# Loads moved to GpSimd's queue, pooled rows in two DRAM tensors, filling rows dropped

## The chip, the cores and the metric

One NeuronCore of a Trainium2 chip. The metric is the device time of one execution in microseconds (us); of several runs the median counts. TensorE does matmuls, transposes among them; VectorE (DVE), ScalarE (ACT) and GpSimd (POOL) work elementwise; SyncE (SP) only issues transfers here. SP, ScalarE and GpSimd can each issue DMAs, which run on the core's 16 DMA engines. Every engine takes its own instructions in order, a DMA issue among them, and waits on semaphores.

## The reference

Inputs are q, k and v of 8 batches, 8 heads, 576 positions and 64 columns (f32), a gate vector, and two matrices of 512 x 1024 and 1024 x 512.

```python
q_d, k_d, v_d = (x.reshape(B, H, S // 4, 4, D).mean(axis=3) for x in (q, k, v))
out_up = np.repeat(sm_attn(q_d, k_d, v_d), 4, axis=2)            # coarse attention, 144 rows
mask = np.abs(pos[:, None] - pos[None, :]) < 4
out_local = softmax(where(mask, scale * q @ k.T, -1e9)) @ v      # local attention
x = (out_up + out_local)  as (B, S, H * D)
scores = einsum("bsd,d->bs", x, w_gate)
for b in range(B):
    top_idx = the 128 rows with the largest scores[b]
    xe = x[b, top_idx]
    ye = np.maximum(xe @ w1, 0) @ w2
    out[b, top_idx] = xe + sigmoid(scores[b, top_idx])[:, None] * ye
```

Each batch has a coarse attention (every pooled row is used for four positions), a local one within three positions, their sum, and a two-layer network on the 128 best rows, which are read from and written back to the output by index.

## The kernel before, in words

The batches run through a software pipeline. Each step of a batch is a Python generator; `put` gives it a place in time in units of a batch (the table `PLACE`), and all pieces are written into the program in the order of these places. The tile framework then sets the semaphores, chooses buffers and orders the instructions of an engine again by its own estimate. Instructions that go through the helper `InOrder` (lines 48 to 55; the names `sp`, `aq`, `vq`) are pinned behind the instruction that the program last gave to the same engine; the profile records them all as line 55.

The steps of batch b:

- `load_qk` (line 169) loads q and k transposed into the tile T in two halves of 1152 KB, more than a batch ahead. `pool_qk` (178) sums groups of four columns on VectorE.
- `pool_v` (202) loads vraw, 1152 KB, and sums groups of four rows on GpSimd (207, 209), into vd; vr (213) follows. `load_vw` (192) loads the windows of v for the local attention in three transfers, two of 520 KB and one of 260 KB.
- `coarse` (223) has two units: scores (237), exponent (262), transposes (275), product (296 to 311). It ends with the tile ods (319): 128 partitions with 512 columns for the first 128 pooled rows, and 64 columns more in which partition h * 16 + c holds row 128 + c of head h. ods is written to the DRAM tile up_d, each row four times: one transfer for the first 128 rows (323) and four, one for each repetition, for the last 16 (328). Then VectorE works out gate scores from ods (332, 336).
- `load_up` (347) reads up_d back as the tiles x: 128 partitions are two blocks of 58 positions, padded to 64 rows each. It has three groups of tiles (0 and 1, 2 and 3, 4) and seven transfers, one of which brings ten rows that fill tile 4 up to 128 partitions.
- `local` (380) has three units: scores (407), maximum (416), exponent (423), transposes (429), product with vw (441), division (451) into the tile t, gate scores (456).
- `sums` (466) adds t to x on GpSimd (469) and stores x to the output, twelve transfers a batch on SP's queue.
- `route` (481) ranks the 576 scores, makes the list idx (528) of the best 128 and gathers these rows (536) from the output into xe, on GpSimd's queue. It runs while the next batch is in its coarse and local steps.
- `moe` (555) multiplies by the two matrices in f16 pairs (564 to 568, 581 to 583), and a scatter (587), also from GpSimd, writes the rows back.
- `load_weights` (142) loads the matrices in eight pieces through the tile stg during the first batch and a half; ScalarE and VectorE convert each piece (146, 147).

All loads of inputs except the first constants are issued by ScalarE (`aq`), all writes and reads of up_d and all stores by SP (`sp`), the gathers and scatters by GpSimd.

Of the kernel before, what the change touches and what calls it, by code (L numbers as in the profile page):

```python
# [11 lines left out]
F32 = mybir.dt.float32  # L12
# [4 lines left out]
ALU = mybir.AluOpType  # L17
# [41 lines left out]
def tile_multires_attention_moe(ctx: ExitStack, tc: tile.TileContext, qk, vw, vp, cs, w_gate, w1, w2, outs):  # L59
# [2 lines left out]
    nc = tc.nc  # L62
    B, _, _, HP, S = qk.shape
    pool = nc.gpsimd
    sp, aq, vq = (InOrder(tc, e) for e in (nc.sync, nc.scalar, nc.vector))
    D = P // 2
    H = 2 * HP
    DM = H * D
# [44 lines left out]
    def load_constants():  # L113
        n = at["first"]
        sp.dma_start(out=cst[:, :n], in_=cs[:, :n])
        for t in (*qzbuf, *pzbuf, first):
            pool.memset(t, 0.0)
        pool.memset(ones, 1.0)
        nc.vector.tensor_copy(identb, ident)
        nc.vector.tensor_copy(mask.rearrange("p e t k -> p (e t k)"), const("mask"))  # L120
        for t in vals:
            nc.vector.tensor_copy(t[:, :, 0], const("tok"))
        nc.vector.tensor_copy(pen, const("pen"))
        nc.vector.tensor_copy(off, const("off"))
        yield
        aq.dma_start(out=wg, in_=w_gate.unsqueeze(0).broadcast_to([P, DM]))
        aq.dma_start(
            out=wgr, in_=w_gate.rearrange("(h d) -> h d", d=D).unsqueeze(1).broadcast_to([H, SR, D])
        )
        aq.dma_start(out=cst[:, n:], in_=cs[:, n:])  # L130
        pool.tensor_copy(first[:, :P], const("first"))
        yield

# [3 lines left out]
    w2l = cpool.tile([P, NF, DM], F16, name="w2l")  # L137

    x_d = outs
    up_d = [dpool.tile([SD, FACTOR, DM], F32, name=f"up_d{b}") for b in range(B)]  # L140

    def load_weights():
        pend = []

        def convert(sv, h_, l_):
            aq.activation(h_, sv, AF.Copy, scale=WS)
            vq.scalar_tensor_tensor(out=l_, in0=sv, scalar=WS, in1=h_, op0=ALU.mult, op1=ALU.subtract)

        for src, hi, lo, n in ((w1, w1h, w1l, DF), (w2, w2h, w2l, DM)):
            for i in range(4):  # L150
                cc = hi.shape[1] // 4
                stg = ld.tile([P, 4 * 256], F32, tag="stg", name="stg", bufs=4)
                sv = stg.rearrange("p (c f) -> p c f", f=n)
                aq.dma_start(
                    out=sv, in_=src[i * cc * P : (i + 1) * cc * P, :].rearrange("(c p) f -> p c f", p=P)
                )
                cs_ = slice(i * cc, (i + 1) * cc)
                pend.append((sv, hi[:, cs_, :], lo[:, cs_, :]))
                if len(pend) == 4:
                    convert(*pend.pop(0))  # L160
                yield
        while pend:
            convert(*pend.pop(0))
            yield
# [4 lines left out]
    def load_qk(b):  # L169
        qkT[b] = wk.tile([P, 2, HP, S], F32, tag="T", name=f"T{b}")  # L170
        hh = HP // 2
        for u in range(2):
            aq.dma_start(
                out=qkT[b][:, :, hh * u : hh * (u + 1)], in_=qk[b][:, :, hh * u : hh * (u + 1)]
            )
            yield
# [15 lines left out]
    def load_vw(b):  # L192
        vwin[b] = []
        for i, tiles in enumerate(TU):
            t = wk.tile([P, 2 * len(tiles), HP, D1], F32, tag=f"vw{i}", name=f"vw{b}_{i}", bufs=1)
            aq.dma_start(out=t, in_=vw[b][:, 2 * tiles[0] : 2 * tiles[-1] + 2])
            vwin[b].append(t)
            yield

# [1 line left out]

    def pool_v(b):
        raw = ld.tile([P, FACTOR, DM + D], F32, tag="vraw", name="vraw", bufs=2)
        aq.dma_start(out=raw, in_=vp[b])
        yield
        vd = vds[b] = wk.tile([P, DM + D], F32, tag="vd", name=f"vd{b}")
        pool.tensor_tensor(out=vd, in0=raw[:, 0], in1=raw[:, 1], op=ALU.add)  # L207
# [15 lines left out]
    def coarse(b):  # L223
# [3 lines left out]
        def unit(u):  # L227
# [76 lines left out]
            for a in range(2):  # L304
# [16 lines left out]
            )  # L321

            sp.dma_start(
                out=up_d[b][:P],
                in_=ods[:, :H, :].rearrange("p h d -> p (h d)").unsqueeze(1).broadcast_to([P, FACTOR, DM]),
            )
            for r in range(FACTOR):
                sp.dma_start(out=up_d[b][P:, r].rearrange("c (h d) -> h c d", d=D), in_=ods[:, H, :])

            su = sm.tile([P, 2], F32, tag="su", name="su")  # L330
            jk = wk.tile([P, DM], F32, tag="jk", name="jk", bufs=1)
# [15 lines left out]
    def load_up(b):  # L347
        uv = up_d[b].rearrange("c r d -> (c r) d")
        xs[b] = []
        for i, tiles in enumerate(TU):  # L350
            x = wk.tile([P, len(tiles), DM], F32, tag=f"x{i}", name=f"x{b}_{i}", bufs=1)
            xs[b].append(x)
            n = 64 if tiles[-1] < NT - 1 else qns[-1]
            for p0, p1, q0 in (
                (0, 64, 2 * QB * tiles[0]), (64, 64 + n, 2 * QB * tiles[0] + QB), (64 + n, P, 0),
            ):
                if p0 < p1:
                    sp.dma_start(
                        out=x[p0:p1],
                        in_=bass.AP(  # L360
                            tensor=uv.tensor, offset=uv[q0, 0:1].offset,
                            ap=[[DM, p1 - p0], [2 * QB * DM, len(tiles)], [1, DM]],
                        ),
                    )
        yield

# [99 lines left out]
    def sums(b):  # L466
        for x, tiles in zip(xs[b], TU):
            for i, j in enumerate(tiles):
                pool.tensor_tensor(out=x[:, i], in0=x[:, i], in1=ts[b][j], op=ALU.add)  # L469
            for e in range(2):  # L470
                n = qns[2 * tiles[-1] + e]
                for p0, p1 in ((0, 48), (48, n)):
# [263 lines left out]
```

## Time and profile before

| | us |
|---|---|
| median of three runs | 380.62 |
| the three runs | 380.48, 380.62, 385.15 |
| the profiled execution | 377.89 |
| its span, first to last instruction | 376.1 |

The mean clock granted to TensorE is 0.841 of full speed. The rows below come from this one execution. Times in rows start at the span's beginning. A row of a timeline has start, length, engine, line, operation, target and source, count, and in square brackets how long the engine idled before it and what ended that. ACTq, SPq and POOLq are the instructions that an engine's sequencer carries out itself, DMA issues above all.

### The profile page before, as it was taken

To read this page: it belongs to the slowest core of one execution; us is meant where nothing else is said; L and a number is where in the kernel's file an instruction comes from. 1 tells how busy PE (TensorE), PEld (TensorE's weight loads), DVE (VectorE), ACT (ScalarE), POOL (GpSimd) and SP (SyncE) were. 2 spreads that over 40 slices of the span, in tenths; PEclk is the share of its full clock that TensorE was granted. 3 is DMA by queue.
4 is the path that set the end of the run, shared out by engine and by line. 5 is a ranking of instruction groups with operands and counts; after the bars stand their busy time and mean duration, and the time that the engine had idled before them with its cause. 6 is when DMAs were issued, how large, how long until landed. Compare 5 with 4: busy or idle time off the path is not lost.

```text
span 376.1 us, 10940 instructions
## 1 busy us (share of the span) xinstructions
PE 287.4 (76%) x4624; PEld 224.8 (60%) x4624; DVE 248.9 (66%) x534; ACT 143.8 (38%) x401; POOL 127.4 (34%) x99
## 2 busy tenths in 40 slices
PE   0680677717799999949996789919997799984984
PEld 0470546606687688638854677619865588673571
DVE  2595867995489777966776658855778667575030
ACT  0541357621445364513623264413624255424010
POOL 1505530471306630753045410733146410351111
PEclk9996556865699999957999599966999589998598
DMA  8897999782686969774777397765687343733100
GB/s 309 294 408 245 281 324 359 256 219 56 218 293 215 251 229 337 202 204 137 262 271 199 106 292 288 190 200 149 240 281 223 86 132 116 200 95 72 28 30 28
DMA packets 32832, 78.25 MB, mean 208 GB/s; under 512 B 7824, under 2 KB 7824, under 8 KB 31760
## 3 DMA queue, kind: packets, MB, share of 16 engines
q10 hardware_dynamic: 11048, 43.72, 33.5%
q1 hardware_dynamic: 20456, 29.65, 28.1%
q0 software_dynamic: 1280, 4.20, 3.5%
q8 instruction: 36, 0.59, 0.6%
q14 instruction: 12, 0.10, 0.1%
HBM read 56.58 MB, written 20.97 MB: 206 GB/s over the span
## 4 chain that ended last, share of the span: by engine, by line
PE 35%; DMA 30%; DVE 14%; issue 10%; ACT 7%; SPq 2%; POOL 1%; ACTq 1%; POOLq 0%; DVEq 0%
DMA up_d<-ods 11%; DMA x<-up_d 7%; DMA xe<-out_dram,idx 6%; ACT ed L262 4%; DMA out_dram<-xe,idx 3%; PE od L296 3%; PE ph L564 3%; PE ol L441 3%; PE ph L567 3%; PE sd L237 2%; PE ph L568 2%; PE pspl L429 2%; DMA T<-in_qk_dram 2%; SPq L55 2%; PE sl L407 2%
## 5 line engine op out<-in xcount | busy, mean ns | idle before, releaser
L469 POOL TENSOR_TENSOR x<-x,t 128x512 f32<-128x512 f32 x40 | 64.5, 1618 | 71.7 <-DVE t L451 55.4
L567 PE MATMUL ph<-xel,w1h 128*128 128x128 f16 x256 | 49.2, 230 | 1.6 <-DVE xel L548 1.6
L564 PE MATMUL ph<-xeh,w1h 128*128 128x128 f16 x256 | 49.7, 231 | 0.8 <-ACT xeh L547 0.7
L207 POOL TENSOR_TENSOR vd<-vraw 128x576 f32<-128x576 f32 x8 | 12.1, 1512 | 111.4 <-DMA vraw<-in_vp_dram 97.3
L568 PE MATMUL ph<-xeh,w1l 128*128 128x128 f16 x256 | 49.1, 230 | 0.0
L441 PE MATMUL ol<-vw,pt 64*64 64x65 f32 x1280 | 33.7, 255 | 19.9 <-DVE den L450 10.1
L55 DVE TENSOR_REDUCE dT<-T 128x288 f32<-128x1152 f32 x32 | 42.8, 1343 | 4.0 <-DMA T<-in_qk_dram 4.0
L441 PEld LDWEIGHTS ol<-vw,pt 64*64 64x64 f32 x1280 | 28.3, 163 | 25.3 <-ACT qz L189 10.4
L429 PE MATMUL pspl<-cst,ex 128*128 128x128 f32 x160 | 28.0, 315 | 11.5 <-ACT ex L423 11.5
L423 ACT ACTIVATE ex<-ex 128x1024 f32<-128x1024 f32 (+1 forms) x24 | 21.9, 913 | 33.3 <-DVE ex L419 17.5
L407 PE MATMUL sl<-T 64*58 64x64 f32 (+1 forms) x1280 | 33.6, 230 | 0.0
L456 DVE SCALAR_TENSOR_TENSOR jk<-t,wg 128x512 f32<-128x512 f32 x40 | 30.4, 763 | 1.0
L451 DVE TENSOR_TENSOR t<-ol,den 128x512 f32<-128x512 f32 x40 | 27.6, 692 | 4.0 <-DVE den L450 0.5
L407 PEld LDWEIGHTS sl<-T 64*58 64x58 f32 (+1 forms) x1280 | 28.2, 138 | 2.7 <-issue 0.8
L431 ACT COPY pt<-pspl 128x512 f32<-128x512 f32 x40 | 22.3, 582 | 19.1 <-PE pspl L429 18.9
L564 PEld LDWEIGHTS <-w1h 128*128 128x128 f16 x256 | 26.9, 105 | 3.1 <-issue 1.9
L429 PEld LDWEIGHTS pspl<-cst,ex 128*128 128x128 f32 x160 | 20.5, 161 | 13.7 <-ACT ex L423 12.0
L568 PEld LDWEIGHTS <-w1l 128*128 128x128 f16 x256 | 26.7, 104 | 2.2 <-issue 1.8
L567 PEld LDWEIGHTS <-w1h 128*128 128x128 f16 x256 | 26.8, 105 | 0.4
L262 ACT ACTIVATE ed<-sd,mxd 128x144 f32<-128x144 f32 x64 | 25.9, 524 | 0.5
L503 DVE SCALAR_TENSOR_TENSOR beat<-srow,scp,first 128x640 bf16<-128x640 f32 (+4 forms) x40 | 25.6, 673 | 0.0
L416 DVE TENSOR_REDUCE mx<-sl 128x16 f32<-128x1024 f32 (+1 forms) x24 | 24.8, 1033 | 1.1 <-PE sl L407 1.1
(132 smaller groups left out, 589.2 us busy)
## 6 DMA issues: line engine op xcount, KB each, us to landing
T<-in_qk_dram ACTq DMA_DIRECT2D x16, 1152.0 KB
vraw<-in_vp_dram ACTq DMA_DIRECT2D x8, 1152.0 KB
vw<-in_vw_dram ACTq DMA_DIRECT2D x16, 520.0 KB
up_d<-ods SPq DMA_DIRECT2D x8, 1024.0 KB
x<-up_d SPq DMA_DIRECT2D x32, 256.0 KB
out_dram<-x SPq DMA_DIRECT2D x32, 192.0 KB
stg<-in_moe_w_dram ACTq DMA_DIRECT2D x8, 512.0 KB
vw<-in_vw_dram ACTq DMA_DIRECT2D x8, 260.0 KB
```

Source lines behind the costliest of these rows:

```text
L55: return lambda *a, **k: self.tc.keep_in_program_order(f(*a, **k))
L262: nc.scalar.activation(ed[:, :, h] if h < H else er, s[:, a, SD * i : SD * (i + 1)], AF.Exp, bias=mx[:, c : c + 1], scale=pscale, accum_ou ...
L407: nc.tensor.matmul(s[64 * e : 64 * e + qn, a, c : c + KW], lhsT=T[64 * a : 64 * a + 64, 0, hp, q0s[blk] : q0s[blk] + qn], rhs=T[64 * a : 6 ...
L429: nc.tensor.transpose(ps[:, hp, :], ex[:, HP * i + hp, :], ident)
L441: nc.tensor.matmul(o[64 * e : 64 * e + 64, a, D1 * hp : D1 * (hp + 1)], lhsT=pt[64 * a : 64 * a + 64, hp, 64 * e : 64 * e + 64], rhs=vl[64 ...
L451: nc.vector.tensor_tensor(out=t.rearrange("p (g a d) -> p a g d", a=2, d=D), in0=ov[:, :, :, 0:D], in1=den.unsqueeze(3).broadcast_to([P, 2 ...
L456: nc.vector.scalar_tensor_tensor(out=jk, in0=t, scalar=1.0, in1=wg, op0=ALU.mult, op1=ALU.mult, accum_out=sc[:, j : j + 1],)
L469: pool.tensor_tensor(out=x[:, i], in0=x[:, i], in1=ts[b][j], op=ALU.add)
L503: nc.vector.scalar_tensor_tensor(out=beat[:, : NT - j].rearrange("p j u -> p (j u)"), in0=sr[:, P * j :], scalar=scp[:, j : j + 1], in1=fi ...
L564: nc.tensor.matmul(ph[:, i, :], lhsT=w1h[:, c, fs], rhs=xeh[:, c, :], start=c == 0, stop=False)
L567: nc.tensor.matmul(ph[:, i, :], lhsT=w1h[:, c, fs], rhs=xel[:, c, :], start=False, stop=False)
L568: nc.tensor.matmul(ph[:, i, :], lhsT=w1l[:, c, fs], rhs=xeh[:, c, :], start=False, stop=c == NC - 1)
```

## The change

All loads that ScalarE issued are issued by GpSimd, through a fourth `InOrder` helper, so they are pinned behind the instruction last given to GpSimd. up_d keeps only the first 128 pooled rows (512 positions); the last 64 positions go to a new DRAM tile rest_d, laid out by head, in one transfer. The reads of x take rows from up_d as far as it goes and the others from rest_d. Tile 4 has 118 used partitions; the filling rows 118 to 127 are not loaded, and its sum covers 118 partitions.

```diff
-    sp, aq, vq = (InOrder(tc, e) for e in (nc.sync, nc.scalar, nc.vector))
+    sp, aq, vq, lq = (InOrder(tc, e) for e in (nc.sync, nc.scalar, nc.vector, nc.gpsimd))
...
-        aq.dma_start(out=wg, in_=w_gate.unsqueeze(0).broadcast_to([P, DM]))
+        lq.dma_start(out=wg, in_=w_gate.unsqueeze(0).broadcast_to([P, DM]))
...
-    up_d = [dpool.tile([SD, FACTOR, DM], F32, name=f"up_d{b}") for b in range(B)]
+    up_d = [dpool.tile([P, FACTOR, DM], F32, name=f"up_d{b}") for b in range(B)]
+    rest_d = [dpool.tile([H, SR * FACTOR, D], F32, name=f"rest_d{b}") for b in range(B)]
...
-            aq.dma_start(
+            lq.dma_start(
                 out=qkT[b][:, :, hh * u : hh * (u + 1)], in_=qk[b][:, :, hh * u : hh * (u + 1)]
             )
...
-            aq.dma_start(out=t, in_=vw[b][:, 2 * tiles[0] : 2 * tiles[-1] + 2])
+            lq.dma_start(out=t, in_=vw[b][:, 2 * tiles[0] : 2 * tiles[-1] + 2])
...
-        aq.dma_start(out=raw, in_=vp[b])
+        lq.dma_start(out=raw, in_=vp[b])
...
             sp.dma_start(
-                out=up_d[b][:P],
+                out=up_d[b],
                 in_=ods[:, :H, :].rearrange("p h d -> p (h d)").unsqueeze(1).broadcast_to([P, FACTOR, DM]),
             )
-            for r in range(FACTOR):
-                sp.dma_start(out=up_d[b][P:, r].rearrange("c (h d) -> h c d", d=D), in_=ods[:, H, :])
+            sp.dma_start(
+                out=rest_d[b].rearrange("h (c r) d -> (h c) r d", r=FACTOR),
+                in_=ods[:, H, :].unsqueeze(1).broadcast_to([P, FACTOR, D]),
+            )
...
-            n = 64 if tiles[-1] < NT - 1 else qns[-1]
-            for p0, p1, q0 in (
-                (0, 64, 2 * QB * tiles[0]), (64, 64 + n, 2 * QB * tiles[0] + QB), (64 + n, P, 0),
-            ):
-                if p0 < p1:
+            for e in range(2):
+                q0 = 2 * QB * tiles[0] + QB * e
+
+                n = min(64, S - 2 * QB * tiles[-1] - QB * e)
+                n0 = min(n, max(0, P * FACTOR - q0 - 2 * QB * (len(tiles) - 1)))
+                if n0:
                     sp.dma_start(
-                        out=x[p0:p1],
+                        out=x[64 * e : 64 * e + n0],
                         in_=bass.AP(
                             tensor=uv.tensor, offset=uv[q0, 0:1].offset,
-                            ap=[[DM, p1 - p0], [2 * QB * DM, len(tiles)], [1, DM]],
+                            ap=[[DM, n0], [2 * QB * DM, len(tiles)], [1, DM]],
                         ),
+                    )
+                if n0 < n:
+                    t0 = q0 + n0 - P * FACTOR
+                    sp.dma_start(
+                        out=x[64 * e + n0 : 64 * e + n, 0].rearrange("p (h d) -> p h d", d=D),
+                        in_=rest_d[b][:, t0 : t0 + n - n0].rearrange("h t d -> t h d"),
                     )
...
-                pool.tensor_tensor(out=x[:, i], in0=x[:, i], in1=ts[b][j], op=ALU.add)
+                n = min(P, 64 + S - 2 * QB * j - QB)
+                pool.tensor_tensor(out=x[:n, i], in0=x[:n, i], in1=ts[b][j][:n], op=ALU.add)
```

The loads of wgr, of the other constants and of stg change from `aq` to `lq` in the same way.

## Rows read from the trace of the kernel before

**Rows 1.** The page, part 1: busy us, share of the span, instructions.
```profile
PE 287.4 (76%) x4624; PEld 224.8 (60%) x4624; DVE 248.9 (66%) x534; ACT 143.8 (38%) x401; POOL 127.4 (34%) x99
```

**Rows 2.** The page, part 4: the chain that ended last, by line.
```profile
DMA up_d<-ods 11%; DMA x<-up_d 7%; DMA xe<-out_dram,idx 6%; ACT ed L262 4%; DMA out_dram<-xe,idx 3%; PE od L296 3%; PE ph L564 3%; PE ol L441 3%; PE ph L567 3%; PE sd L237 2%; PE ph L568 2%; PE pspl L429 2%; DMA T<-in_qk_dram 2%; SPq L55 2%; PE sl L407 2%
```

**Rows 3.** Stretches: length; busy PE, PEld, DVE, ACT, POOL; clock, DMA share, GB/s.
```profile
28.00:38.00 10.00, 1.51 (x36) 1.37 (x27) 5.60 (x13) 2.00 (x2) 5.71 (x4) 0.67 0.73 252
38.00:48.00 10.00, 5.46 (x113) 4.45 (x111) 8.44 (x15) 3.25 (x6) 5.62 (x4) 0.50 1.05 282
48.00:77.00 29.00, 22.57 (x340) 18.03 (x340) 23.73 (x44) 18.37 (x49) 8.21 (x6) 0.70 0.87 303
77.00:87.00 10.00, 0.59 (x3) 0.62 (x4) 7.27 (x12) 1.39 (x4) 5.15 (x4) 0.61 0.89 231
...
130.00:160.00 30.00, 28.82 (x505) 22.25 (x505) 25.38 (x54) 15.31 (x44) 11.74 (x9) 1.00 0.79 255
```

**Rows 4.** Timeline of ScalarE, first batch and fourth: load issues and stalled work.
```profile
35.44 0.34 ACTq L55 DMA_DIRECT2D stg<-in_moe_w_dram  x1
35.82 1.06 ACT L423 ACTIVATE ex<-ex 128x1024 f32<-128x1024 f32 x1 [9.33 <-DMA up_d<-ods]
...
46.46 0.34 ACTq L55 DMA_DIRECT2D vw<-in_vw_dram  x1
...
47.36 1.06 ACT L55 ACTIVATE w1h<-stg 128x1024 f16<-128x1024 f32 x1 [5.94 <-DMA x<-up_d]
...
144.98 0.37 ACTq L55 DMA_DIRECT2D vraw<-in_vp_dram  x1
...
158.14 0.34 ACTq L55 DMA_DIRECT2D vw<-in_vw_dram  x1
```

**Rows 5.** The chain that ended last in order of time: start, length, piece.
```profile
0.74 0.66 ACTq L55
...
24.23 10.73 DMA up_d<-ods
...
38.36 8.08 DMA x<-up_d
```

**Rows 6.** Timeline of VectorE: the ends of four rankings, and one weight conversion.
```profile
74.81 0.15 DVE L528 CAST idx<-pi 128x1 int32<-128x1 f32 x1
...
76.72 1.65 DVE L55 SCALAR_TENSOR_TENSOR w2l<-stg,w2h 128x1024 f16<-128x1024 f32 x1
...
160.42 0.15 DVE L528 CAST idx<-pi 128x1 int32<-128x1 f32 x1
...
204.44 0.16 DVE L528 CAST idx<-pi 128x1 int32<-128x1 f32 x1 [2.03 <-DMA out_dram<-xe,idx]
...
249.14 0.16 DVE L528 CAST idx<-pi 128x1 int32<-128x1 f32 x1 [4.42 <-DMA out_dram<-xe,idx]
```

**Rows 7.** Timeline of GpSimd: last memset, two gathers, first sum of vd.
```profile
2.10 0.09 POOL L118 MEMSET ones<- 128x1 bf16 x1
...
77.45 1.95 POOL L536 DMA_INDIRECT xe<-out_dram,idx  x1 [0.17 <-DMA x<-up_d]
...
150.72 1.61 POOL L207 TENSOR_TENSOR vd<-vraw 128x576 f32<-128x576 f32 x1 [13.73 <-DMA vraw<-in_vp_dram]
...
162.53 0.98 POOL L536 DMA_INDIRECT xe<-out_dram,idx  x1 [0.15 <-issue]
```

**Rows 8.** Instructions of tile idx: gather issue in ns (min/median/max); landing of gathers, scatters.
```profile
L536 POOL DMA_INDIRECT xe<-out_dram,idx x8: 972/984/1948, 77.5 to 350.4; - x8
...
DMA to landing us min/median/max: 2.7/4.6/8.8
```

**Rows 9.** Instructions of tile up_d, 147 to 162 us: ns min/median/max, first and last start.
```profile
L55 SPq DMA_DIRECT2D up_d<-ods x5: 570/756/1397, 148.4 to 152.2; - x5
```

**Rows 10.** The page, parts 3 and 6: SP's queue, and the loads of T.
```profile
q1 hardware_dynamic: 20456, 29.65, 28.1%
...
T<-in_qk_dram ACTq DMA_DIRECT2D x16, 1152.0 KB
```

More of the change, by code (lines that the diff above doesn't have):

```diff
@@ L125, in load_constants @@
         yield
-        aq.dma_start(out=wg, in_=w_gate.unsqueeze(0).broadcast_to([P, DM]))
-        aq.dma_start(
+        lq.dma_start(out=wg, in_=w_gate.unsqueeze(0).broadcast_to([P, DM]))
+        lq.dma_start(
             out=wgr, in_=w_gate.rearrange("(h d) -> h d", d=D).unsqueeze(1).broadcast_to([H, SR, D])
         )
-        aq.dma_start(out=cst[:, n:], in_=cs[:, n:])
+        lq.dma_start(out=cst[:, n:], in_=cs[:, n:])
         pool.tensor_copy(first[:, :P], const("first"))
@@ L153, in load_weights @@
                 sv = stg.rearrange("p (c f) -> p c f", f=n)
-                aq.dma_start(
+                lq.dma_start(
                     out=sv, in_=src[i * cc * P : (i + 1) * cc * P, :].rearrange("(c p) f -> p c f", p=P)
@@ L172, in load_qk @@
         for u in range(2):
-            aq.dma_start(
+            lq.dma_start(
                 out=qkT[b][:, :, hh * u : hh * (u + 1)], in_=qk[b][:, :, hh * u : hh * (u + 1)]
```

## The prediction

> **What bounds the kernel now.** I read the page's busy shares first, then the chain of waits, then tables of stretches, and at the end the timelines of single engines. No engine fills the span: TensorE is busy 76% of 376.1 us [rows 1]. The chain goes through three transfers, up_d written 11%, x read back 7%, the gather of xe 6% [rows 2]. So the time is made of hand-overs as much as of work. The stretches show two kinds [rows 3]. From 130 to 160 us all is well: TensorE 28.82 of 30 us, VectorE 25.38 (85%), clock 1.00 (the full 2.4 GHz). From 28 to 48 us TensorE has 6.97 busy us of 20, and its clock there is 0.67 and 0.50; from 48 to 77 us it is busy but at 0.70.
>
> The hole from 28 to 48 us has a cause that the change touches. ScalarE idles 9.33 us before L423's exponent, and 5.94 us before a weight conversion [rows 4]. Directly ahead of the first stands a load of stg on ScalarE's queue, which went out at 35.44; the five writes of up_d had landed at 24.23 + 10.73 = 34.96 [rows 5]. Directly ahead of the second, loads went out when the read of x from 38.36 had landed, at 46.44. No data ties stg to up_d or x. I infer that the loads wait for a completion counter which they share with SP's transfers, and that everything behind them on ScalarE waits too. 9.33 + 5.94 = 15.3 us.
>
> In the batches after that, the gather of the batch before is late. In the second batch idx is done at 74.81 + 0.15 = 74.96 [rows 6] and the gather starts at 77.45 [rows 7], 2.49 us later; in the fourth it is 160.57 and 162.53, 1.96 us. In the fifth and sixth idx itself starts 2.03 and 4.42 us late, behind the landing of the scatter [rows 6]. Together 10.9 us; TensorE has little to do meanwhile (0.59 busy us from 77 to 87 us [rows 3]), since gathers and scatters take 4.6 us at the median to land [rows 8].
>
> **The change, part by part.** *The start.* The first load of T goes out at 0.74 now [rows 5]. On GpSimd it is traced behind the memsets, whose last ends at 2.10 + 0.09 = 2.19 [rows 7]: +1.45 us. A GpSimd issue of 128 rows took 0.98 us at the median, once 1.95 [rows 8]; ScalarE's took 0.66 [rows 5]. The second half of T is therefore later by 1.45 + 0.32 = 1.8 us, at the slow issue by 1.45 + 2 x 1.95 - 2 x 0.66 = 4.0. The chain starts with T, so nothing hides it. I take +2.0, bounds +1.5 and +4.0.
>
> *The hole from 28 to 48 us.* With the loads on another queue ScalarE no longer stands behind them, so up to 15.3 us go. VectorE is late next: from 28 to 77 us it has 5.60 + 8.44 + 23.73 = 37.8 busy us [rows 3]. Filled entirely, that saves 49 - 37.8 = 11.2; at the 85% of the good stretch it is 44.5 us, a saving of 4.5. The lower bound is nothing, since the DMA engines are busy 0.73 to 1.05 there and may be the next limit. I take -8.0, between the two readings of VectorE.
>
> *The pooled rows and SP's queue.* Five writes become two, so three issues of 0.76 us at the median [rows 9] fall out, 2.3 us a batch; and the reads of the first four ranges need only the one large write. Reads stay seven a batch, as the filling rows go and the last tile's first half is cut in two. GpSimd's sum of the first tiles thus starts up to 2.3 us earlier, and the gather queued behind it too. The vraw load helps in the same place: it goes out at 144.98 on ScalarE behind a vw load and that engine's work [rows 4], and GpSimd then idles 13.73 us before vd [rows 7]. On GpSimd's own queue it can go as soon as that engine has nothing ahead of it. Both act on the 10.9 us of late gathers, and can give no more than these; a landing that comes no earlier gives 0. I take half, -5.5.
>
> *The rest rows.* The last tile's rows come in pieces of 256 B: per batch 128 + 432 = 560 pieces instead of 80 rows of 2 KB. SP's packets took 28.1% of 16 x 376.1 us over 20456, 83 ns each [rows 10]; 560 of them over 16 engines are 2.9 us a batch of all engines at most. Only the sum of the last tile waits for them, which comes after its t. I count 0; uncovered in all eight batches it is +23, a bound that needs the last sum to set every period. The 118 instead of 128 partitions of that sum change nothing in its length.
>
> *The issues on GpSimd.* 16 + 8 + 24 + 8 + 3 = 59 loads at 0.98 us are 58 us on top of 127.4 [rows 1], 49% of the span: GpSimd doesn't become the bound. What matters is who stands behind: sums, scatter and gather. A vw load goes out shortly ahead of the gather (158.14, the gather at 162.53 [rows 4, 7]); on one engine it costs the gather 0.98 us of issue. In three of seven batches I count that, +3.0; bounds 0, and 7 x 1.95 = +13.7.
>
> The one slow issue [rows 7] ran beside VectorE's w2l, which reads two SBUF tiles and lasted until 76.72 + 1.65 = 78.37 [rows 6]; from there to its end it had the usual 1.0 us. [...]
>
> Sum: +2.0 - 8.0 - 5.5 + 3.0 = -8.5. The profiled execution took 377.89 us, so 369.4; the median of the runs, 380.62, is 0.7% above it, so 372.1, say 372.
>
> **The rivals.** *The start is limited anyway.* DMA share 0.73 and 1.05 between 28 and 48 us speaks for it, VectorE's idle third against. Then the -8.0 falls away: 377.89 + 2.0 - 5.5 + 3.0 = 377.4, on the median 380.
>
> *The gather queues behind loads (slower).* Now the gather has a queue of its own beside ScalarE's and SP's. After the change T, vraw, vw, gather and scatter use one. With a 1152 KB load of T or vraw ahead [rows 10] the 256 KB gather waits for 1408 KB; sharing alternately it would have waited for about 512. The difference of 896 KB at 230 GB/s (the stretch from 77 to 87 us moved 231 [rows 3]) is 3.9 us, with the issue 4.9. In five batches +24.5: 377.89 + 2.0 - 8.0 - 5.5 + 24.5 = 390.9, on the median 394. Against it: only vw, not T or vraw, goes out just ahead of the gather now. It passes the 2% line from four batches on. The Trainium skill, "DMA: Bandwidth & Descriptors", sections "Queues, rings and completion order" and "SWDGE vs HWDGE vs iDMA", says that an engine alternates between the queues that have work and that GpSimd has a single one. By that rule this rival's order is what any load ahead of the gather meets; no run so far shows two GpSimd transfers in one queue.
>
> *Everything that waits goes.* 11.2 us in the hole, and the 22.57 busy us of TensorE from 48 to 77 us [rows 3] at clock 1.00 instead of 0.70, 15.8, are 6.8 more; 10.9 at the gathers, no cost on GpSimd: 377.89 + 2.0 - 28.9 = 351, on the median 353. VectorE at 100% speaks against.
>
> *No decoupling.* If the loads on GpSimd still wait for SP's transfers, the sums wait behind them in place of ScalarE; this is the first rival's time or worse, and I count it there.
>
> **How the numbers follow.** The forecast (366 to 378 on the median) has 0.45, the limited start 0.20, the gather behind loads 0.18, everything going 0.17. Measurement tells about 2% from no change: below 373.0 faster, above 388.2 slower. Faster: 0.33 of the forecast and 0.17 make 0.50. Slower: 0.18, and 0.03 of the limited start with costs on top, 0.21. Same: the rest, 0.29. The range runs from 355, just above the best case, to 391, a gather behind loads in some four batches; about 0.1 lies outside on either side. The 23 us of uncovered pieces would lie beyond and is left out as unlikely. The likeliest case's own range is 366 to 378.
>
> **What would show it.** Right: ScalarE's waits of 9.33 and 5.94 us gone and the clock above 0.67 between 28 and 48 us; VectorE above 80% there; GpSimd's loads near 1 us each; SP's reads of x beginning some 2 us sooner after ods; landing of gathers and scatters still near 4.6 us. Wrong: a landing of 7 us and more (the slower rival); ScalarE waiting for stg or w1h data in the first 50 us (the limited start); GpSimd's loads at 2 us; sums waiting for the last x.

## The result and the profile after

The changed kernel takes 381.44 us (median of 20 runs, 379.13 to 384.13); the kernel before took 377.86 beside it (20 runs, 374.27 to 385.15). The ratio is 1.012, with an interval of 1.009 to 1.015: about 1.2% slower, inside the 2% that count as no change, where the forecast was 372 and faster. The same kernel on two chips can shift by about one per cent against its neighbour (e1: 0.994 and 1.000, e5: 0.992 and 1.004). Of b2, e9, e11, the first run of e1 and the second of e6 only a slow, disturbed execution was profiled, so their rows serve for waits, single starts and the drain, not for whole times.

The profiled execution took 381.3 us with a span of 379.5 (before: 377.89 and 376.1). First the busy shares of the page, part 1, which answer to [rows 1]:

```profile
PE 291.2 (77%) x4624; PEld 226.4 (60%) x4624; DVE 258.0 (68%) x534; ACT 143.2 (38%) x401; POOL 165.2 (44%) x158
```

GpSimd has 38 us more, VectorE 9 more. Next the stretches of the kernel after, with the columns of [rows 3] (length; busy us of each engine; clock, DMA share, GB/s):

```profile
0.00:28.00 28.00, 13.67 (x217) 10.35 (x217) 11.94 (x19) 8.49 (x29) 16.14 (x30) 1.00 0.62 224
28.00:38.00 10.00, 2.98 (x12) 2.50 (x12) 5.88 (x9) 4.70 (x8) 0.40 (x2) 0.61 1.02 399
38.00:48.00 10.00, 3.45 (x109) 3.08 (x113) 3.11 (x9) 1.06 (x1) 5.46 (x5) 0.53 0.89 285
48.00:77.00 29.00, 17.59 (x294) 13.11 (x290) 25.11 (x45) 13.04 (x36) 15.11 (x15) 0.71 0.87 302
77.00:87.00 10.00, 7.46 (x120) 6.70 (x119) 9.83 (x20) 5.43 (x12) 6.11 (x4) 0.72 0.65 200
...
130.00:160.00 30.00, 28.71 (x528) 22.53 (x528) 24.67 (x56) 13.62 (x42) 13.47 (x14) 1.00 0.83 263
```

The hole from 28 to 48 us is still there: TensorE has 6.43 busy us in it, where [rows 3] have 6.97. VectorE went from 14.04 to 8.99. The first line is new: the DMA engines are busy for 0.62 of the first 28 us. The same stretch of the kernel before:

```profile
0.00:28.00 28.00, 14.50 (x270) 11.25 (x274) 16.25 (x27) 9.89 (x33) 7.10 (x15) 1.00 0.90 337
```

The timeline of GpSimd (it answers to [rows 7]) says why, kernel after:

```profile
2.14 1.65 POOL L55 DMA_DIRECT2D T<-in_qk_dram  x2
3.79 0.56 POOL L55 DMA_DIRECT2D vraw<-in_vp_dram  x1
13.96 1.40 POOL L208 TENSOR_TENSOR vd<-vraw 128x576 f32<-128x576 f32 x1 [9.61 <-DMA vraw<-in_vp_dram]
15.44 2.89 POOL L210 TENSOR_TENSOR vd<-vd,vraw 128x576 f32<-128x576 f32 x2
18.27 0.59 POOL L55 DMA_DIRECT2D wg<-in_moe_w_gate_dram  x1
...
21.07 0.77 POOL L55 DMA_DIRECT2D T<-in_qk_dram  x1
...
27.58 0.53 POOL L55 DMA_DIRECT2D vw<-in_vw_dram  x1 [1.54 <-DMA T<-in_qk_dram]
```

Three loads are issued; then the sum vd, which waits for vraw, stands ahead of all others: from 4.35 to 18.27 us nothing is requested from DRAM. The first windows, which ScalarE had requested at 4.97, are requested last, at 27.58, and contend with everything that came late together. The chain of waits and TensorE's timeline show the end of it, kernel after:

```profile
27.58 15.85 DMA vw<-in_vw_dram
```

```profile
43.47 2.01 PE L451 MATMUL ol<-vw,pt 64*64 64x65 f32 x64 [6.71 <-DMA vw<-in_vw_dram]
```

ScalarE's two waits of [rows 4] behind SP's transfers are gone as forecast, but the hole has another owner. The issues are cheaper than forecast; groups of instructions, kernel after (busy us, mean ns of one):

```profile
L55 POOL DMA_DIRECT2D vw<-in_vw_dram x24 | 13.5, 562 | 1.5 <-DMA T<-in_qk_dram 1.5
L55 POOL DMA_DIRECT2D T<-in_qk_dram x16 | 11.8, 737 | 0.0
L55 POOL DMA_DIRECT2D stg<-in_moe_w_dram x8 | 5.1, 641 | 0.0
```

The instructions of the tile idx, kernel after (they answer to [rows 8]):

```profile
L547 POOL DMA_INDIRECT xe<-out_dram,idx x8: 971/1147/1615, 92.1 to 351.6; - x8
...
DMA to landing us min/median/max: 2.8/4.0/5.8
```

Gathers and scatters land in 4.0 us at the median, not in 7 or more: one shared GpSimd queue does not make them land late here. VectorE's casts of idx no longer wait for a scatter (2.03 and 4.42 us in [rows 6]).

Where did 3.4 us of span come from? I follow the batches by the starts of ods (lines 319 and 320) and by the last scatter, which starts at the same 371.55 us in both:

| us | before | after | difference |
|---|---|---|---|
| first ods | 23.44 | 28.58 | +5.1 |
| first to second ods | 43.63 | 48.40 | +4.8 |
| second to last ods | 248.48 | 237.53 | -11.0 |
| last ods to last scatter | 56.00 | 57.04 | +1.0 |
| last scatter to end of span | 4.55 | 7.95 | +3.4 |

So in this pair of executions nothing is lost or won in the sum up to the last scatter. The whole difference lies behind it. The last instructions of GpSimd's queue, by line (ns min/median/max, first and last start), before and then after:

```profile
L730 POOLq DRAIN  x3: 40/102/3678, 371.3 to 375.5; - x3
```

```profile
L741 POOLq DRAIN  x3: 46/97/7432, 371.3 to 379.3; - x3
```

GpSimd's closing drain takes 7.43 instead of 3.68 us: +3.75, of which 3.4 show in the span, beside a difference of medians of 381.44 - 377.86 = 3.6. That the terms before the drain cancel so exactly is one pair of executions; the experiments have to show whether it holds.

### The profile page after: what moved, and what is told of

Same layout as the page of the kernel before. It is cut to its first block, busy times and chain, and to the rows that moved or that the text cites. A ratio compares the mean times of both kernels' runs of the same rounds, so it can differ in the third digit from the quotient of the medians.

```text
span 379.5 us, 10896 instructions
## 1 busy us (share of the span) xinstructions
PE 291.2 (77%) x4624; PEld 226.4 (60%) x4624; DVE 258.0 (68%) x534; ACT 143.2 (38%) x401; POOL 165.2 (44%) x158
## 2 busy tenths in 40 slices
DMA packets 35336, 78.09 MB, mean 206 GB/s; under 512 B 12112, under 2 KB 12112, under 8 KB 34264
## 3 DMA queue, kind: packets, MB, share of 16 engines
q0 software_dynamic: 11072, 47.91, 35.1%
## 4 chain that ended last, share of the span: by engine, by line
PE 34%; DMA 21%; DVE 19%; issue 11%; ACT 8%; POOL 4%; SPq 1%; POOLq 0%; DVEq 0%
DMA xe<-out_dram,idx 5%; DMA up_d<-ods 4%; DMA vw<-in_vw_dram 4%; ACT ed L263 4%; PE ol L451 3%; PE sd L238 3%; DMA x<-up_d 3%; DMA vraw<-in_vp_dram 3%; DVE dT L55 3%; PE ph L575 3%; PE pspl L439 2%; PE ph L578 2%; DVE beat L514 2%; PE ph L579 2%; PE od L297 2%
## 5 line engine op out<-in xcount | busy, mean ns | idle before, releaser
L480 POOL TENSOR_TENSOR x<-x,t 128x512 f32<-128x512 f32 (+1 forms) x40 | 65.0, 1629 | 69.8 <-DVE t L461 38.1
L451 PE MATMUL ol<-vw,pt 64*64 64x65 f32 x1280 | 35.4, 257 | 22.9 <-DVE den L460 7.1
L451 PEld LDWEIGHTS ol<-vw,pt 64*64 64x64 f32 x1280 | 29.1, 164 | 29.0 <-issue 15.0
L417 PE MATMUL sl<-T 64*58 64x64 f32 (+1 forms) x1280 | 34.6, 234 | 0.0
L439 PE MATMUL pspl<-cst,ex 128*128 128x128 f32 x160 | 29.2, 324 | 5.0 <-ACT ex L433 5.0
L466 DVE SCALAR_TENSOR_TENSOR jk<-t,wg 128x512 f32<-128x512 f32 x40 | 31.9, 796 | 1.0
L417 PEld LDWEIGHTS sl<-T 64*58 64x58 f32 (+1 forms) x1280 | 29.1, 141 | 3.0 <-issue 1.1
L514 DVE SCALAR_TENSOR_TENSOR beat<-srow,scp,first 128x640 bf16<-128x640 f32 (+4 forms) x40 | 29.4, 768 | 0.0
L238 PE MATMUL sd<-dT 64*128 64x144 f32 x128 | 19.2, 420 | 9.6 <-DVE dT L55 9.2
L439 PEld LDWEIGHTS pspl<-cst,ex 128*128 128x128 f32 x160 | 21.3, 165 | 7.6 <-ACT ex L433 5.2
```

The source lines that it names most:

```text
L238: nc.tensor.matmul(s[:, a, SD * i : SD * (i + 1)], lhsT=dT[64 * a : 64 * a + 64, 0, hp, :P], rhs=dT[64 * a : 64 * a + 64, 1, hp, :], start ...
L417: nc.tensor.matmul(s[64 * e : 64 * e + qn, a, c : c + KW], lhsT=T[64 * a : 64 * a + 64, 0, hp, q0s[blk] : q0s[blk] + qn], rhs=T[64 * a : 6 ...
L439: nc.tensor.transpose(ps[:, hp, :], ex[:, HP * i + hp, :], ident)
L451: nc.tensor.matmul(o[64 * e : 64 * e + 64, a, D1 * hp : D1 * (hp + 1)], lhsT=pt[64 * a : 64 * a + 64, hp, 64 * e : 64 * e + 64], rhs=vl[64 ...
L466: nc.vector.scalar_tensor_tensor(out=jk, in0=t, scalar=1.0, in1=wg, op0=ALU.mult, op1=ALU.mult, accum_out=sc[:, j : j + 1],)
L480: pool.tensor_tensor(out=x[:n, i], in0=x[:n, i], in1=ts[b][j][:n], op=ALU.add)
```

## The experiments

### One part at a time

e1 takes the rows' part of the change without the loads, e2 the loads without the rows.

```diff
# e1, on the changed kernel, at all seven places
-        lq.dma_start(
+        aq.dma_start(
# e2, on the kernel before, at all seven places
-        aq.dma_start(
+        lq.dma_start(
```

> The new handling of the pooled rows alone, all loads issued by ScalarE as before. Theory A (the change wins in the batches after the first and loses some 10 us before the second ods, because the first windows of v are loaded last on GpSimd's queue): the second ods lies near 67 us as before, not 77; ScalarE's waits behind SP's transfers (9.3 and 5.9 us) are still there; the time is at or below that of the kernel before, ratio 0.98 to 1.00. Theory B (the loads' new queue slows every batch): the same here, so this run gives only the rows' own share. Rival C (the 256-byte pieces cost something in each batch): ratio above 1.01, and sums wait longer for x.

> All loads issued by GpSimd, the pooled rows as before. Theory A: the second ods near 77 us again, ScalarE's two waits behind SP's transfers gone, the first windows of v landing after 40 us; ratio 1.00 to 1.03. If the steady gain comes from the rows alone, the ratio is at its upper end, near 1.03 (loss of 10 us and no gain); if it comes from the loads, near 1.01, as the whole change. Theory B: each batch after the second ods longer than before, ratio above 1.03.

e1 gave 0.994 (0.989 to 0.999) and, repeated on another chip, 1.000 (0.995 to 1.004); e2 1.016 (1.011 to 1.021). The rows' part makes no difference that I can show; the loads make the loss. The drain is 3.68 us in e1 and 7.43 in e2.

> The pooled rows' part alone once more, in five rounds, since the version with stg on GpSimd gave 0.992 on one chip and 1.004 on another: if the part is worth something by itself, the ratio is 0.988 to 0.998; if the first result was a matter of the chip, the interval holds 1.

### The order of the first loads

e3 leaves the first windows, both gate vectors and the constants on ScalarE; e4 keeps GpSimd and gives constants and windows earlier places.

```diff
# e3; wg, wgr and cst go back to aq in the same way
-            lq.dma_start(out=t, in_=vw[b][:, 2 * tiles[0] : 2 * tiles[-1] + 2])
+            (lq if b else aq).dma_start(out=t, in_=vw[b][:, 2 * tiles[0] : 2 * tiles[-1] + 2])
# e4, in PLACE
-    "CS": (0.6, 0.1),
+    "CS": (0.3, 0.1), ("VW", 0): (0.1, 0.2),
```

> The changed kernel with the first batch's windows of v and the constants wg, wgr, cst issued by ScalarE; everything else on GpSimd. Theory A: TensorE no longer waits for the first windows (landing before 30 us instead of 43.5), the second ods 7 to 12 us earlier than in the changed kernel, the time 5 to 12 us less: ratio to before 0.975 to 0.995. Theory B: less than 3 us gained, ratio above 1.00.

> The changed kernel with everything still on GpSimd, but the first batch's windows of v and the constants given places ahead of the first sums of vd. Theory A (order within the queue, not the queue itself): the same gain as with ScalarE within 4 us, ratio to before 0.975 to 0.995. Rival D (it takes a second queue, as transfers of one queue stand behind each other): the windows land early but T of the second batch late; gain under half of that of the run with ScalarE.

e3 gave 1.038 (1.033 to 1.043), e4 1.016 (1.010 to 1.022). In e4 the second ods starts at 69.12 instead of 76.98, but the next six periods take 247.9 us instead of 237.5: 8 us won at the start and more than given back. My theory that the start alone carries the loss fell here: both ratios missed the 0.975 to 0.995 that it asked for. Both runs also showed a confounder: moving a load makes the framework order the instructions of every engine anew, and these two kernels differ from the changed one in more than the loads.

### The queue apart from the order

The order goes with the engine that issues the loads: on the four engines that compute, e1 has the instructions in the order of before, e2 in that of the changed kernel. So I held the order. In a3 the kernel before issues its loads from GpSimd, with all other work held to the order of before; in b2 it issues them from ScalarE, held to the order of e2. b5 and a5 do the same to the changed kernel: b5 has its loads on ScalarE, a5 on GpSimd at places that the framework chooses, both with all other work in the order of the changed kernel.

```diff
-    sp, aq, vq, lq = (InOrder(tc, e) for e in (nc.sync, nc.scalar, nc.vector, nc.gpsimd))
+    sp, aq, vq = (InOrder(tc, e) for e in (nc.sync, nc.scalar, nc.vector))
+    lq = nc.gpsimd        # a3 and a5; b2 and b5 issue by aq
...
+        for a, b in zip(want, want[1:]):      # neighbours on each engine, loads left out
+            if a and b:
+                tc.add_manual_dep(
+                    known[f"I-{b}"], f"I-{a}",
+                    mybir.DependencyInfo(mybir.DependencyClass.NoSync, mybir.DependencyReason.DATA), reason="order",
+                )
```

> The kernel before with its loads on GpSimd, and the order of TensorE's, VectorE's, ScalarE's, SP's and GpSimd's own work held to that of before by order-only edges. Theory Q (issuing on GpSimd costs time by itself, at the drain and at the start): the last drain reads about 7.4 us as in the loads-only run, ods starts near 23 to 25 and then keeps within 3 us of before's 67, 112, 148, 190, 232, 276, 316; the time is 3 to 6 us above before, ratio 1.008 to 1.016. Theory O (the loads alone cost nothing, the other order of instructions that the framework chose does it): ratio 0.995 to 1.003. Theory P (ScalarE freed of its waits, as the prediction had it): the first period after the first ods shortens by 5 us or more and the ratio is below 0.99.

> The kernel before with its loads on ScalarE as before, but the order of all other work held to that of the loads-only run. Theory Q (the queue): the drain is back at 3.68 us and the first windows land early, so the time is 4 to 8 us under the loads-only run's 383.1, near 376 to 379. Theory O (the order): ods starts near 29 and 77 as in the loads-only run, the middle from the second to the last ods takes 238 to 240 us, and the time is within 4 us of the loads-only run, 379 to 384.

> The changed kernel with its loads issued by ScalarE again, all other work of all engines held to the order of the changed kernel. Theory Q (the queue): the drain is 3.68 instead of 7.43 us, the first windows go out early and the DMA engines are busy 0.85 or more in the first 28 us (0.62 in the changed kernel), the second ods is near 70 to 73 instead of 77, and the time is 4 to 7 us under the changed kernel's 1.012 of before, ratio 0.993 to 1.002. Theory O (the order of the instructions): the second ods stays at 75 or later, only the drain is won, ratio 1.002 to 1.010.

> The changed kernel with its loads still on GpSimd, but not pinned in program order: the framework places them, all other work held to the order of the changed kernel. Drain 7.43 us again. If the loads that stand behind the first sums on GpSimd are what makes the second ods late (DMA engines busy 0.62 in the first 28 us) and that lateness lasts to the end, an earlier place brings it to 67 to 72 and the time 4 to 9 us down, ratio 0.988 to 1.003. If a late start is made good by the middle anyway, as with the loads in the order of before (first ods 10.6 us late, last scatter 0.1), the ratio stays 1.006 to 1.016 whatever the second ods does.

| loads issued by | order of before | order of e2 | changed kernel and its order |
|---|---|---|---|
| ScalarE | 1 (before) | 1.002, 0.998 to 1.007 (b2) | 1.002, 0.997 to 1.006 (b5) |
| GpSimd | 1.009, 1.005 to 1.014 (a3) | 1.016, 1.011 to 1.021 (e2) | 1.012, 1.009 to 1.015 (after) |

Read down each column: the queue costs 0.9, 1.4 and 1.0%, that is 3.5 to 5.1 us of 378. Only the first column is known to be from one chip, so it is the one that counts; the others agree with it, no more. Read along the upper row: the order costs nothing that can be measured in the sum. In a3 the profile shows it step by step. Its first ods starts at 34.01, 10.6 us late; it makes this good over the periods (first 40.93 instead of 43.63, second 41.93 instead of 44.94, sixth 41.15 instead of 43.74, seventh 38.75 instead of 39.85), and the last scatter starts at 371.67, 0.12 us behind before. The span is 3.5 us longer all the same. GpSimd's timeline and its drain, kernel a3:

```profile
371.67 0.97 POOL L588 DMA_INDIRECT out_dram<-xe,idx  x1 [11.45 <-DVE xe L587]
```

```profile
L731 POOLq DRAIN  x3: 46/97/7412, 371.4 to 379.4; - x3
```

Theory Q holds with its main price at the end, not with the punctual start near 23 to 25 that I had expected of it. In the changed kernel's order the start may cost something too: b5's last scatter starts at 363.74, 7.8 us before the changed kernel's. But b5's profiled execution took 369.98 us beside a median of 376.86, so I read no price from it. What the order does is also seen: the first period is 48.4 us in the changed kernel and 48.5 in b5, 43.6 in before. The casts of idx wait for scatters in before and a3, and in neither e2 nor b5. From the instructions of tile idx, kernel a3, and then its landing in the same view of b5:

```profile
  DVE idx L529: 7.1, 3
DMA to landing us min/median/max: 2.7/5.1/8.3
```

```profile
DMA to landing us min/median/max: 2.7/4.7/6.1
```

The first line is missing in b5. So the late second ods and the missing scatter waits come with this order, whichever engine issues the loads. The early windows of b5 did not shorten its first period: ScalarE stands behind stg again there, and TensorE waits. ScalarE's timeline, kernel b5:

```profile
33.30 2.23 ACTq L55 DMA_DIRECT2D stg<-in_moe_w_dram  x2
35.58 1.06 ACT L55 ACTIVATE w1h<-stg 128x1024 f16<-128x1024 f32 x1 [8.88 <-DMA rest_d<-ods]
36.54 1.04 ACT L433 ACTIVATE ex<-ex 128x1024 f32<-128x1024 f32 x1
```

In b5 and in the changed kernel two different waits thus leave a hole of the same length.

a5 was a miss: 1.036 (1.030 to 1.042). Its first ods starts at 34.38, 5.8 us behind the changed kernel's; the second, at 78.00, is only 1.0 behind, but the last scatter, at 381.55, is 10.0 behind. So most of the late start is made good, and the loss comes later: the fourth period takes 47.97 instead of 42.91. In it GpSimd stands before a load of vw whose buffer TensorE has not yet released, and the sums x and vd stand behind that load. a5's loads also show that GpSimd's queue is not free of the coupling of [rows 4]. GpSimd's timeline, kernel a5, first the coupling and last the wait for the buffer:

```profile
13.99 0.54 POOL L156 DMA_DIRECT2D stg<-in_moe_w_dram  x1 [2.23 <-DMA vraw<-in_vp_dram]
15.27 0.54 POOL L198 DMA_DIRECT2D vw<-in_vw_dram  x1 [0.74 <-DMA stg<-in_moe_w_dram]
16.55 0.53 POOL L206 DMA_DIRECT2D vraw<-in_vp_dram  x1 [0.74 <-DMA stg<-in_moe_w_dram]
19.40 0.53 POOL L198 DMA_DIRECT2D vw<-in_vw_dram  x1 [2.32 <-DMA T<-in_qk_dram]
...
191.99 0.55 POOL L198 DMA_DIRECT2D vw<-in_vw_dram  x1 [12.18 <-PE ol L452]
```

Loads into different tiles wait for the landing of earlier loads of the same queue, and the sums behind them wait too: the first sum of vd starts at 23.22, in the changed kernel at 13.96.

### What the drain grows with

e7 and e8 are the kernel before with 59 more transfers on GpSimd into a tile that nothing reads.

```diff
+        for k in range(8 * b, min(8 * b + 8, 59)):
+            nc.gpsimd.dma_start(out=extra[0:1, k : k + 1], in_=cs[0:1, k : k + 1])   # e8: extra[:, k : k + 1]
```

> The kernel before with 59 extra transfers on GpSimd of one 4-byte piece each, into a tile that nothing reads, eight with each vraw load. If the last drain grows with the number of transfers that GpSimd issued (16 + 59 = 75, as in the changed kernel), it reads 7.4 us; if with packets (1280 + 59) or bytes, it stays near 3.7. The whole time is not the question: about 4 us of issue per batch stand ahead of GpSimd's own work.

> The same 59 transfers, each of 128 pieces of 4 bytes: 7552 more packets, only 30 KB. If the drain grows with packets, it reads 3.68 + 7552 x 0.00038 = 6.6 us here and 3.7 in the run with single pieces; if with transfers, 7.4 in both; if with bytes, 3.7 in both.

Page, part 3, of e7 (packets, MB, share) and its drain:

```profile
q0 software_dynamic: 3168, 4.20, 3.6%
```

```profile
L733 POOLq DRAIN  x3: 51/103/7426, 395.6 to 403.5; - x3
```

With 3168 packets and 4.2 MB the drain is that of the changed kernel, which has 11072 packets and 47.91 MB; e8 reads 7.42. (e8 was meant to add 7552 packets, but its page shows the 3168 of e7, so it is a repetition of e7.) Neither packets nor bytes set the drain, but the number of transfers that GpSimd issued. The counts of all runs: 16 transfers 3.68 us, 17 (e9) 3.73, 24 (e5) 4.02, 40 (e11) 4.66, 48 (e6, e10) 5.21, 69 (e3) 6.93, 75 7.43 (seven kernels). That is 40 to 50 ns for each up to 40, and 69 to 84 above. An extra transfer of four bytes took 527 ns of GpSimd, hardly less than the 562 for a load of vw of 260 or 520 KB: the issue has a price of its own, whatever it moves. The whole times of these two, 405.57 and 403.44 us, come from the start: the 59 issues all fall into the first 50 us, among the first sums of vd (first ods at 53.54 in e7). They are not the question.

### What the hole from 28 to 48 us is worth

e5 is e1 with the loads of stg alone on GpSimd. e9 is e5 with only the first of eight weight pieces loaded, which all conversions then read; seven pieces of 512 KB are left out.

```diff
# e5, on e1, in load_weights
-                aq.dma_start(
+                lq.dma_start(
# e9, on e5
+                if len(stgs) < 1:
+                    stgs.append(ld.tile([P, 4 * 256], F32, tag="stg", name="stg", bufs=4))
...
```

> The pooled rows' part of the change alone, with only the eight loads of stg on GpSimd and the others on ScalarE. If the drain grows with every transfer that GpSimd issued, it reads 3.68 + 8 x 0.064 = 4.2 us here. ScalarE's waits of 9.33 and 5.94 us, which stood behind a load of stg and loads issued after it, should shrink; if that fills the hole from 28 to 48 us as the prediction said, the second ods comes 5 us or more before the 71.9 of the rows-only run and the time is 370 to 374. If something else is late there (the rival: VectorE and the transfers themselves), the time stays at the rows-only run's 0.994 of before, within 0.006.

> The version with the pooled rows' part and stg alone on GpSimd once more, in five rounds, as the best so far: ratio to before 0.986 to 0.996, faster than both kernels with an interval that does not reach 1.

> The pooled rows' part with stg on GpSimd, but only the first of the eight weight pieces is loaded, and all eight conversions read it; the other seven (7 x 512 KB = 3.7 MB) are left out. Theory D (the first 77 us are limited by the DMA engines, which move 311 GB/s there): 3.7 MB are 11.8 us, so the second ods and the first ranking come 8 to 12 us earlier than 67.4 and 79.3, and the time is 361 to 367, ratio 0.955 to 0.975. Theory V (VectorE and the hand-overs between engines set the hole): the second ods comes less than 4 us earlier and the ratio is 0.98 to 0.995.

e5 gave 0.992 (0.987 to 0.996) and, repeated, 1.004 (0.999 to 1.010): no gain that holds. ScalarE's waits of 8.73 and 5.98 us in e1 (repeated) shrink to one of 5.08 behind a load of vw, and the second ods starts at 67.36 and 66.89, against 67.86 in e1 (repeated): 0.5 to 1.0 us. In e10 (below) the last of these waits is gone too, and the second ods starts at 66.65, against 67.07 in before. That is what I had priced at 8. In e6, where these waits are gone as well, the second ods starts at 70.09 and 67.86, no earlier than in e1, so the steps say only that the price is small. What takes the place of these waits is the landing of stg itself, for which ScalarE waits 4.98 and 5.26 us in e6; ScalarE's timeline, kernel e10:

```profile
31.40 1.06 ACT L55 ACTIVATE w1h<-stg 128x1024 f16<-128x1024 f32 x1 [5.05 <-DMA stg<-in_moe_w_dram]
```

e9 gave 0.986 (0.978 to 0.994), where e5 gave 1.004 on the same chip, with the second ods at 62.96. Without 3.7 MB, which would take 11.8 us at 311 GB/s (the rate of e5's first 77 us), 4 us come back. The stretch of the hole, e5 repeated and then e9:

```profile
28.00:48.00 20.00, 7.96 (x184) 6.48 (x184) 14.51 (x26) 5.84 (x9) 12.45 (x11) 0.70 0.90 256
```

```profile
28.00:48.00 20.00, 7.90 (x184) 6.33 (x184) 17.54 (x31) 6.10 (x11) 13.34 (x8) 0.69 0.74 201
```

With most of ScalarE's wait out of the way the transfers are next (share 0.90); with these relieved too (0.74) VectorE is, at 17.54 of 20 us. TensorE's busy time does not change at all. So I read three limits that stand nearly level in the hole: taking the first away is worth about 1 us at the second ods, and the first two 67.86 - 62.96 = 4.9. That VectorE is the third is argued from its busy share; no run relieves it.

### A version that beats both

e6 is e5 with the windows vw on GpSimd too (T, vraw and constants on ScalarE). e10 is the same without the rows' part, e11 the same with stg back on ScalarE.

```diff
# e6, on e5; e10 has the same two edits on the kernel before
-            aq.dma_start(out=t, in_=vw[b][:, 2 * tiles[0] : 2 * tiles[-1] + 2])
+            lq.dma_start(out=t, in_=vw[b][:, 2 * tiles[0] : 2 * tiles[-1] + 2])
# e11, on e6, in load_weights
-                lq.dma_start(
+                aq.dma_start(
```

> As the run before it, with the 24 loads of vw on GpSimd as well; T, vraw and the constants stay on ScalarE, so the first sums of vd no longer wait ahead of loads of constants, and only vw and stg stand behind them. Drain 3.68 + 32 x 0.064 = 5.7 us. If the first windows landing last is what makes the second ods late, it is late here too (74 to 78) and the time is 1.000 to 1.012 of before; if the windows are issued early enough, the second ods is at 67 to 70 and the ratio is 0.98 to 1.00.

> The pooled rows with stg and vw on GpSimd once more, in five rounds: as the best candidate 0.980 to 0.996 of before. If its 0.986 came from few runs on one chip, the interval holds 1.

> The kernel before with stg and vw on GpSimd, the pooled rows as before. The version with the rows' part gave 0.988 of before, the rows' part alone 1.000 and 0.994. If the gain is that of moving the windows and weights, the ratio is 0.985 to 0.996 here; if the two parts must come together, it is 0.997 or more. Drain 5.2 us either way.

> The rows' part with vw alone on GpSimd, stg back on ScalarE: 16 + 24 = 40 transfers, so a drain of about 4.8 us by the values at 24 and 48. If vw carries the gain, the ratio is 0.984 to 0.994; if ScalarE's waits behind stg matter too, it is 0.995 or more.

e6 gave 0.986 (0.974 to 0.998) and on another chip 0.988 (0.983 to 0.993); e10 0.991 (0.986 to 0.996). e6 beats the kernel before on two chips, by less than 2%, although its drain costs 1.53 us more. e10 does so on one chip only, as e5 did before its repetition gave 1.004; that the gain doesn't need the rows' part is likely but not shown. e11 gave 1.021 (1.015 to 1.027), on the side that I had named for waits behind stg that matter, but with a loss that I hadn't expected. ScalarE's timeline, kernel e11:

```profile
34.39 2.11 ACTq L55 DMA_DIRECT2D stg<-in_moe_w_dram  x2
36.55 1.06 ACT L433 ACTIVATE ex<-ex 128x1024 f32<-128x1024 f32 x1 [9.56 <-DMA rest_d<-ods]
...
46.67 1.06 ACT L55 ACTIVATE w1h<-stg 128x1024 f16<-128x1024 f32 x1 [4.96 <-DMA x<-rest_d]
```

With stg back, the waits of [rows 4] are back, and in e6 and e10 they are absent: the load behind SP's transfers is the cause of these waits, as the prediction inferred. The trace of before has the counter itself: SP's and ScalarE's transfers signal the same eight semaphores in turn. The write of up_d that went out at 25.67 signals number 101 for the last time at 35.42, and the load of stg that waits for this number goes out at 35.44. GpSimd's transfers have eight semaphores of their own. But e11 is 3% slower than e6, and e1, which has waits of 8.73 and 5.98 us in these places, is not. The instructions of e11 stand in another order too. How much of e6's gain is the moved loads and how much the order that came with them I did not separate.

## Why the prediction was wrong

**The start.** I took +2.0 with bounds of +1.5 and +4.0; it was +5.1 at the first ods. The path that I had priced was right: TensorE's last product for ods ends at 25.18 instead of 23.40, 1.8 us later. The other 3.3 us are VectorE's, which has a sum of the second batch's T ahead of ods; VectorE's timeline, kernel after:

```profile
27.31 1.35 DVE L55 TENSOR_REDUCE dT<-T 128x288 f32<-128x1152 f32 x1 [3.33 <-DMA T<-in_qk_dram]
```

The halves of this T were requested at 21.07 and 22.38, behind the sum vd, and at 14.68 and 17.13 before. I asked only what a load costs the sums, scatters and gathers behind it, and not what a sum that waits for vraw does to the loads behind it. That also put the first windows at 27.58 and left the DMA engines at 0.62 of the first 28 us.

**The hole from 28 to 48 us.** This is the step of the sum that failed: -8.0 was taken, and the first period came out 4.8 us longer. The mechanism I inferred was right (the two waits of [rows 4] go with stg and vw, as e10 and e11 show), its price was not: e5 and e10 put it at 0.4 to 1.0 us, and e6 shows no gain there. I had VectorE as the next limit at 11.2 or 4.5 us and noted a DMA share of 0.73 to 1.05 only as a lower bound of nothing. That bound was the value to take. The same order with the loads on ScalarE (b5) has a first period just as long, 48.5 us.

**The pooled rows and the late gathers.** The reads of x started sooner after ods, but by 0.65 us on the mean of batches two to eight, not by 2.3, and 3.5 us later in the first. The -5.5 looked right in the sum, since the middle gave 11 us, but for another reason: the scatter waits went with the order of instructions (absent in e2 and b5, present in a3), not with earlier transfers. The rows' part alone is worth nothing measurable.

**The rest rows.** Counted at 0; e1 agrees. Packets under 512 B went from 7824 to 12112 (12224 in e1) at no price that can be measured.

**The issues on GpSimd.** I took 0.98 us from the gather, and +3.0 in the sum; plain loads took 0.54 to 0.74 on the mean of a group. The one large cost of issuing there was not in the sum at all: 59 transfers lengthen the closing drain by 3.75 us. I looked at what GpSimd's issues would delay and never at what ends the span. The drain of 3.68 us stood in the trace of before, behind the last scatter, where nothing follows that could hide it, and I didn't ask what it depends on.

**The rivals.** *The start is limited anyway* gave 380 and lies nearest, and e9 shows its limits; but its sum arrives there without the drain, with a start too cheap and with a middle that came out differently, so the number is luck in good part. *The gather queues behind loads* did not come about: gathers and scatters landed in 4.0 us. *Everything that waits goes* is refuted by the hole. *No decoupling* is refuted as it stands, since GpSimd's loads share no semaphore with SP's transfers; but in a5 they wait for each other's landing.

Of what would show it right: ScalarE's two waits went, and gathers land in 4.0 us. Of the rest, clock (0.61 and 0.53) and VectorE (0.59 and 0.31) in the hole, the issues near 1 us and the reads of x 2 us sooner were wrong. Of what would show it wrong, ScalarE's waits for stg came, 1.11 and 2.12 us before 40 us: the sign of the limited start.

The Trainium skill, "DMA: Bandwidth & Descriptors", section "Issuing engine by pattern", gives simple loads to the SP queue and indirect ones to GpSimd. No run here issues the input loads from SP. Against ScalarE's queue the runs agree for a whole kernel of plain loads on GpSimd (0.9 to 1.4% lost by the queue alone), and not for a part of them: e6 moves 32 there and wins 1.2 to 1.4%, with an order of instructions that may have a share in it.

## What to carry to other kernels

Before you move transfers to an engine, follow both directions in its queue: what waits behind them, and what that engine already waits for ahead of them, since an engine that sums what it loads stops requesting while it waits. Then look at the last instructions of the span and ask what each depends on; a cost that nothing can hide counts in full, while gains in the middle are shared between limits that stand level. Where a tool orders instructions anew after every edit, hold the order in a control run, or you price the order and call it the edit.

## What was not expected of the hardware

GpSimd's closing drain grows with the number of transfers that GpSimd issued (3.68 us at 16, 5.21 at 48, 7.43 at 75), and neither with their packets nor their bytes. A plain transfer takes 0.53 to 0.74 us of GpSimd to issue on the mean of its group, four bytes or 1152 KB, where an indirect one of 128 rows takes 0.97 and more. And the shift of a kernel from chip to chip is as large as the effects here: the same kernel (e5) came out at 0.992 and 1.004 of the same neighbour, so a single result below one per cent says little until a second chip repeats it.
